# Attention and two MoE stages on one core: one pair's sums on VectorE, weight subtractions outside the routing chains, first keys in two PSUM tiles

## The chip, the cores and the metric

The kernel runs on one core of one Trainium2 chip. The metric is the device time of one execution in microseconds (us); lower is better. Inside the core five engines work side by side and meet through semaphores: TensorE (PE, matmuls and transposes), VectorE (DVE), ScalarE (ACT), GpSimd (POOL) and SyncE (SP, which only issues DMAs here). Matmul results land in PSUM, everything else lies in SBUF.

## The reference

Three steps, each on what the one before it gave:

```python
# 1 attention with random features, 16 heads (2 x 8) of 576 rows x 64
k_p, q_p = phi(k), phi(q)            # exp(x @ omega.T - sq - max) / sqrt(m), 128 features
kv, z = k_p.T @ v, k_p.sum(rows)     # per head
x = (q_p @ kv) / (q_p @ z + 1e-6)    # -> 1152 tokens x 512
# 2 MoE: 8 experts, top 1, room for 288 tokens each
logits = x @ w_gate; e = argmax(logits); gate = softmax(logits)[e]
y = relu(disp[e] @ w1[e]) @ w2[e]    # 512 -> 1024 -> 512
x = gate * y[e, pos]                 # dropped tokens give 0
# 3
h = max(x @ w1, x @ w2, x @ w3)      # 512 -> 768
out = h @ w_out                      # 768 -> 512
```

## The kernel before, in words

The order of the work is written out by hand: every engine runs its instructions in the order in which the program emits them, and an instruction whose input is not ready holds up all behind it on its engine. A list `fill` of generators (routing, transposes and lists) is advanced by one piece at each `step()`, so that their work falls between the matmuls of the main stream.

**Attention.** Two heads make a pair; there are eight pairs (`NPR`), four for each half of the tokens (`b` = 0, 1). Per pair, `proj` (L237) projects keys (s = 0) and queries (s = 1) on omega into PSUM, four tiles of 128 rows for each head, and `proj_half` the last 64 rows. `minimum` (L254) takes the row minimum on VectorE, L256, and `feature` (L258) the exponential on ScalarE, L261. `sums` (L286) adds the four key tiles of each head, L293 and L295, on the engine that the letter in the table `SUMS` (L45) names: VectorE for pair 0, GpSimd for the others. `kv_mm` (L297, matmuls L302) builds the 64 x 128 product, `z_mm` (L312) uses the sums, `q_t` (L330) transposes the query features into `qps` (L334) and ScalarE copies them out, `num` (L340) forms numerator and denominator, divides on VectorE (L356 to L379) and writes the rows into X. `keep` sends X to DRAM as XD.

**Routing.** `route(b, ...)` (L427) runs once for each half: logits, argmax, one-hot, counts by a matmul `rp` (L454), a chain of small VectorE instructions (L461 to L513) that chooses an expert and gives each token a place, five comparisons `pm` (L516, one per token tile), 15 matmuls `vps` (L534) that turn them into row indices, the indices (L558, L559), and three indirect DMAs on GpSimd (L543) that gather the rows of the expert from XD. `expert_reg` reads the expert's number into SP's register and issues the loads of its weights. The first routing is spread over pairs 5 to 7, the second over the end of the attention and the first expert's matmuls. `route_rest` picks the small third expert; its list needs the matmuls at L610. `transpose_rows` (L832) turns the gathered rows with PE into `tps` (L837), four tiles of three transposes each; ScalarE casts xth, VectorE subtracts xtl (L829).

**Experts.** Weights come as 512 KB pieces. `split` (L776) makes of a piece `raw` a rounded `hi` (ScalarE, L785) and the rest `lo` (VectorE, L788); with `split(True)` the subtraction goes into a list `rest`, from which `split_rest` takes one. `stage1` (L842) multiplies by w1 in three products (hi·hi, hi·lo, lo·hi: L140 to L142), ScalarE takes hh, VectorE takes hl (L860); `stage2` by w2. One unit of a stage is 12 matmuls of 288 columns. `tick` (L917) ends a unit; while `early[0]` holds it calls `pump`, and so `split`, only if at least `HOLD` units of the first expert's stage 1 are left. In stage 2 of the first expert the transposes of the second expert's rows start with unit `S0`. `job_c` does the third expert with few rows; the table `CAT` says behind which units of the second expert and of the last MoE its pieces run; in it `cy` (L1138) multiplies by the craw weights, the first half in one piece, the second in the next.

**The last MoE** computes the three products, takes the maximum and multiplies by w_out; its weights are decoded from 16-bit words (L677, L681). Rows are scattered by GpSimd at the end.

The lines that the change touches beside the tables: `proj`, `minimum` and `feature`, `first_keys` (L951), `route` at L521 and L546, and the main loop from L998 to L1041. In the main loop the pieces of the routing sit in `step()`:

```python
            step()
            step()
        else:
            a_step()
        num(i, None if more else lambda: next(r1))
```

## Time and profile before

| | us |
|---|---|
| median of 3 runs | 234.28 |
| lowest and highest | 232.54, 236.75 |
| the profiled execution's own time | 232.21 |
| its span, first to last instruction | 230.2 |
| busy: PE, DVE, ACT, POOL | 216.3, 143.7, 109.8, 51.0 |

The profile is of one execution. The span leaves out some 2 us around it. Busy times of engines overlap each other, and matmuls are pipelined, so PE's busy time includes matmuls that run slower than they could. PE's mean granted clock over the span was 0.986 of full speed.

### The profile page before, as it was taken

The page shows a single profiled execution, that of the slowest core. Times are in us where ns is not written, and L with a number is a line of the kernel's source. Part 1 is how long each engine was busy: PE and PEld are TensorE (multiplying, and loading weights), DVE is VectorE, ACT ScalarE, POOL GpSimd, SP SyncE. Part 2 cuts the span into 40 slices and gives each one's busy share as a digit, 9 for nine tenths or more (in the row PEclk, how much of TensorE's full clock was granted, in tenths as well). Part 3 has the DMA queues.
Part 4 walks back from the last instruction along what each step waited for, and adds up shares of the span by engine and source line. Part 5 has one row for each costly group of instructions (what it writes and reads, how often), then busy time and mean ns, then how long its engine had stood idle before and what let it go on. Part 6 is the DMA issues. An engine that isn't in the chain of part 4 may idle for free. (4 is left out here: it accounts for less than half of the span.)

```text
span 230.2 us, 5130 instructions
## 1 busy us (share of the span) xinstructions
PE 216.3 (94%) x1924; PEld 199.0 (86%) x1924; DVE 143.7 (62%) x379; ACT 109.8 (48%) x268; POOL 51.0 (22%) x96
## 2 busy tenths in 40 slices
PE   7899999999899999899899998999999999999970
PEld 3789998989796999888899997999999999988870
DVE  0755665888979789868898768456944552421120
ACT  2795966884779643046778657336621310000000
POOL 7022523331358021311000000131321111013120
PEclk9999999999979999999999999999999999999997
DMA  5938759991981616979978679974300000001211
GB/s 120 335 102 283 229 177 355 321 323 59 374 330 65 201 51 226 352 246 344 401 278 273 202 245 329 358 240 160 129 4 0 0 3 0 0 1 48 91 48 30
DMA packets 17613, 42.22 MB, mean 183 GB/s; under 512 B 2269, under 2 KB 8797, under 8 KB 17584
## 3 DMA queue, kind: packets, MB, share of 16 engines
q1 hardware_dynamic: 16016, 39.36, 49.2%
q0 software_dynamic: 800, 2.44, 3.1%
q8 instruction: 17, 0.28, 0.5%
q10 hardware_dynamic: 768, 0.05, 0.2%
q14 instruction: 12, 0.10, 0.1%
HBM read 34.36 MB, written 7.54 MB: 182 GB/s over the span
## 5 line engine op out<-in xcount | busy, mean ns | idle before, releaser
L788 DVE TENSOR_TENSOR lo<-raw,hi 128x1024 fp32r<-128x1024 f32 x27 | 33.4, 1242 | 17.5 <-ACT hi L785 15.4
L140 PE MATMUL m<-YH,hi 128*128 128x288 f32 (+1 forms) x144 | 43.3, 301 | 0.0
L141 PE MATMUL m<-YL,hi 128*128 128x288 f32 (+1 forms) x144 | 43.0, 299 | 0.0
L142 PE MATMUL m<-YH,lo 128*128 128x288 f32 (+1 forms) x144 | 42.9, 298 | 0.0
L785 ACT CAST hi<-raw 128x1024 fp32r<-128x1024 f32 x28 | 29.1, 1051 | 26.0 <-PE m L141 11.3
L140 PEld LDWEIGHTS m<-YH,hi 128*128 128x128 f32 x144 | 27.1, 188 | 0.4 <-issue 0.4
L142 PEld LDWEIGHTS m<-YH,lo 128*128 128x128 f32 x144 | 27.1, 188 | 0.0
L141 PEld LDWEIGHTS m<-YL,hi 128*128 128x128 f32 x144 | 27.1, 188 | 0.0
L261 ACT ACTIVATE kp<-ps,mn 128x128 f32<-128x128 f32 x56 | 15.3, 382 | 16.6 <-DVE mn L256 12.1
L677 ACT CAST e<-w 128x512 f16<-128x512 bf16 x24 | 18.7, 785 | 8.8 <-DMA w<-in_wm_dram 8.1
L256 DVE TENSOR_REDUCE mn<-ps 128x4 f32<-128x512 f32 (+1 forms) x32 | 19.4, 650 | 4.3 <-PE ps L249 4.2
L141 PE MATMUL hps<-xtl,hi 128*128 128x288 f32 x64 | 19.0, 297 | 0.7 <-DVE xtl L829 0.7
L140 PE MATMUL y<-hh,hi 128*128 128x288 f32 x64 | 19.6, 306 | 0.0
L1193 DVE TENSOR_TENSOR mxt<-m,mxt 128x288 f32<-128x288 f32 (+1 forms) x24 | 11.1, 462 | 13.4 <-PE m L142 13.0
L140 PE MATMUL hps<-xth,hi 128*128 128x288 f32 x64 | 19.3, 302 | 0.0
L141 PE MATMUL y<-hl,hi 128*128 128x288 f32 x64 | 18.8, 294 | 0.0
L142 PE MATMUL y<-hh,lo 128*128 128x288 f32 x64 | 18.8, 294 | 0.0
L142 PE MATMUL hps<-xth,lo 128*128 128x288 f32 x64 | 18.8, 294 | 0.0
L249 PEld LDWEIGHTS ps<-om,qk 64*128 64x128 f32 x240 | 15.8, 206 | 3.3 <-DVE om L941 1.4
L249 PE MATMUL ps<-om,qk 64*128 64x128 f32 x240 | 17.5, 299 | 1.0 <-DMA qk<-in_qk_dram 0.6
L681 DVE SCALAR_TENSOR_TENSOR raw<-w,e 128x512 int32<-128x512 int32 x24 | 17.0, 714 | 2.3 <-ACT e L677 2.3
L1196 POOL TENSOR_TENSOR H2L<-mxt,H2H 128x288 fp32r<-128x288 f32 (+1 forms) x10 | 9.5, 948 | 38.7 <-ACT H2H L95 23.9
(231 smaller groups left out, 444.5 us busy)
## 6 DMA issues: line engine op xcount, KB each, us to landing
w<-in_wm_dram SPq DMA_DIRECT2D x18, 512.0 KB, 4.9
raw<-in_w_dram SPq DMA_DIRECT2D x16, 512.0 KB, 6.5
qk<-in_qk_dram SPq DMA_DIRECT2D x7, 640.0 KB, 4.3
craw<-in_w_dram SPq DMA_DIRECT2D x8, 512.0 KB, 9.2
w<-in_wo_dram SPq DMA_DIRECT2D x6, 512.0 KB, 4.3
va<-in_va_dram SPq DMA_DIRECT2D x8, 320.0 KB, 4.8
out_dram<-zt SPq DMA_DIRECT2D x9, 256.0 KB, 5.1
XD<-X SPq DMA_DIRECT2D x2, 960.0 KB, 6.3
```

The lines of the kernel that those rows point to most:

```text
L140: T.matmul(ps, lhsT=wh, rhs=xh, start=start, stop=False)
L141: T.matmul(ps, lhsT=wh, rhs=xl, start=False, stop=False)
L142: T.matmul(ps, lhsT=wl, rhs=xh, start=False, stop=stop)
L249: T.matmul(ps[h][:, t, :], lhsT=qk_t[i][r, s, 128 * t:128 * t + 128], rhs=om[r], start=True, stop=True, tile_position=(64 * h, 0),)
L256: V.tensor_reduce(MN[i][:, k + t0:k + t1], PJ[i, s][h][:, t0:t1, :], axis=AX.X, op=ALU.min)
L261: A.activation(dst[:, 4 * h + t, :], PJ[i, s][h][:, t, :], AF.Exp, bias=mn[:, k + t:k + t + 1], scale=-1.0)
L677: A.copy(e.bitcast(F16).rearrange("p (c two) -> p c two", two=2)[:, :, 1], src.bitcast(BF16)[:, 4:4 * WH + 4:4])
L681: V.scalar_tensor_tensor(dst.bitcast(I32), src[:, 1:2 * WH + 1:2], 13, e, ALU.logical_shift_right, ALU.bitwise_or)
L785: A.copy(hi, raw)
L788: (G if SUBS[n] == "G" else V).tensor_tensor(lo, raw, hi, ALU.subtract)
L1193: V.tensor_tensor(mv, p, mv, ALU.max)
L1196: engine(HLS[k]).tensor_tensor(H2L[:, fc, n0:n1], mv, H2H[:, fc, n0:n1], ALU.subtract)
```

## The change

`SUMS[6]` becomes "V": the seventh pair's sums move from GpSimd to VectorE, and their place in the program from before the query minima to behind the two `step()` calls that end the features, ahead of `num`. In `first_keys` pair 0's key tiles t = 0, 1 get one PSUM tile and t = 2, 3 two others, and features follow each half's minima. Of the weight splits in front of the last two pairs, one subtraction is emitted at once and one is taken in the last pair, between `z_mm` and `q_th`; the last pair pumps three times in place of twice. `HOLD` = 9 stops the splits in the ticks of the first expert's stage 1, and two `split()` calls come into the second routing, behind the comparisons and behind the gathers. `S0` = 3 starts the second expert's transposes one unit earlier, and `CAT[1]` starts with 2 and 4 in place of 1 and 3, so two pieces of the third expert come one unit later.

```diff
--- before.py
+++ after.py
@@ -36,12 +36,12 @@
 W1, W2 = 2, 1
 LE, LW = 2, 3
 RA, RB, RM = 0, 1, 1
-R0, S0, LG1, LV, PMG = 4, 4, 4, (0, 3), ()
-ERX, HOLD, NB = (1, 2), 2, 2
+R0, S0, LG1, LV, PMG = 4, 3, 4, (0, 3), ()
+ERX, HOLD, NB = (1, 2), 9, 2
 WARM, CP = 7, (0, 0, 1, 1, 2)
 LI, LL = 7, 8
-CAT = (8, 12, 14), (1, 3, 5, 6)
-SUMS = "VGGGGGGG"
+CAT = (8, 12, 14), (2, 4, 5, 6)
+SUMS = "VGGGGGVG"
 KTS = "AAAAAAAA"
 QTS = "AAAAAAAAAAAAAAAA"
 QHS = "VVVVVVVV"
@@ -236,30 +236,31 @@
 
     def proj(i, s):
 
-        if (i, s) == (1, 0):
+        if i + s == 0 or (i, s) == (1, 0):
 
             nb = pn.tile([128, 2, 512], F32, tag="nb", name="nb")
             ps = [nb[:, h].rearrange("p (t m) -> p t m", m=M) for h in range(2)]
         else:
             ps = [psum([128, 4, M], f"ps{h}") for h in range(2)]
-        PJ[i, s] = ps
+        ps2 = [psum([128, 4, M], f"ps{h}") for h in range(2)] if i + s == 0 else ps
+        PJ[i, s] = (ps, ps, ps2, ps2)
         for t in range(4):
             for h in range(2):
                 r = slice(64 * h, 64 * h + 64)
                 T.matmul(
-                    ps[h][:, t, :], lhsT=qk_t[i][r, s, 128 * t:128 * t + 128], rhs=om[r], start=True, stop=True,
+                    PJ[i, s][t][h][:, t, :], lhsT=qk_t[i][r, s, 128 * t:128 * t + 128], rhs=om[r], start=True, stop=True,
                     tile_position=(64 * h, 0),
                 )
 
     def minimum(i, s, h, t0=0, t1=4):
         k = 8 * s + 4 * h
-        V.tensor_reduce(MN[i][:, k + t0:k + t1], PJ[i, s][h][:, t0:t1, :], axis=AX.X, op=ALU.min)
+        V.tensor_reduce(MN[i][:, k + t0:k + t1], PJ[i, s][t0][h][:, t0:t1, :], axis=AX.X, op=ALU.min)
 
     def feature(i, s, h, tiles=range(4)):
         mn, dst, k = MN[i], (KP, QP)[s][i], 8 * s + 4 * h
         for t in tiles:
             A.activation(
-                dst[:, 4 * h + t, :], PJ[i, s][h][:, t, :], AF.Exp, bias=mn[:, k + t:k + t + 1], scale=-1.0
+                dst[:, 4 * h + t, :], PJ[i, s][t][h][:, t, :], AF.Exp, bias=mn[:, k + t:k + t + 1], scale=-1.0
             )
 
     def proj_half(i):
@@ -519,6 +520,7 @@
         if b == 0:
             V.tensor_copy(KC[:, 0], KT[:, 0])
         if b:
+            split()
 
             expert_reg(b, NB)
         for _ in range(LV[b]):
@@ -544,6 +546,8 @@
                 rows[:n, i], None, XD[:, :], IND(IX[b][:n, i:i + 1], 0), bounds_check=2 * XR - 1, oob_is_err=False
             )
         ROWS[b] = rows
+        if b:
+            split()
         for _ in range(ERX[b] - 1):
             yield
         if b:
@@ -950,12 +954,12 @@
 
     def first_keys():
         proj(0, 0)
-        for t in (0, 2):
+        for t0 in (0, 2):
             for h in range(2):
-                minimum(0, 0, h, t, t + 2)
-        for t in range(4):
-            for h in range(2):
-                feature(0, 0, h, (t,))
+                minimum(0, 0, h, t0, t0 + 2)
+            for t in (t0, t0 + 1):
+                for h in range(2):
+                    feature(0, 0, h, (t,))
 
     def first_rest():
         proj(0, 1)
@@ -998,14 +1002,16 @@
         q_t(i, 1)
         z_mm(i)
         step()
+        if not more:
+            split_rest()
         q_th(i)
         kv_t(i)
         step()
         if i == NPR - 2:
-            for _ in range(2):
-                split(True)
+            split()
+            split(True)
         if not more:
-            for _ in range(2):
+            for _ in range(3):
                 pump()
         if more:
             if i:
@@ -1027,18 +1033,19 @@
                 if i:
                     minimum(nx, 0, h)
                 feature(nx, 0, h)
-            split_rest()
             minimum_half(nx)
             feature_half(nx)
-            sums(nx)
+            if SUMS[nx] == "G":
+                sums(nx)
             for h in range(2):
                 minimum(nx, 1, h)
                 feature(nx, 1, h)
-            split_rest()
             if i == NPR - 2:
                 split()
             step()
             step()
+            if SUMS[nx] == "V":
+                sums(nx)
         else:
             a_step()
         num(i, None if more else lambda: next(r1))
```

VectorE in the first routing. `pm` are the comparisons, `dn` is the denominator of `num`, `ks` and `ksum` are the sums. Before:

```order
L256 TENSOR_REDUCE mn<-ps_940 128x4
L513 SCALAR_TENSOR_TENSOR sm_959<-sm_959,RG 128x5
L516 TENSOR_SCALAR pm<-io,sm_959 128x288 x5
L520 COPY KC<-KT 128x8
L356 TENSOR_SCALAR dn_149<-nb 128x2x4
L357 TENSOR_SCALAR dn_149<-nb 64x2
L358 RECIPROCAL dn_149<-dn_149 128x10
```

and now:

```order
L257 TENSOR_REDUCE mn<-ps_941 128x4
L514 SCALAR_TENSOR_TENSOR sm_960<-sm_960,RG 128x5
L517 TENSOR_SCALAR pm<-io,sm_960 128x288 x5
L521 COPY KC<-KT 128x8
L294 TENSOR_TENSOR ks<-kp 128x512
L296 TENSOR_TENSOR ksum<-ks 128x256
L357 TENSOR_SCALAR dn_149<-nb 128x2x4
L358 TENSOR_SCALAR dn_149<-nb 64x2
L359 RECIPROCAL dn_149<-dn_149 128x10
```

The two sums stand between the comparisons and `num`; the rest keeps its order.

VectorE in the second routing, from hl of stage 1 (L860, now L864) to the first reduction behind the counts, before:

```order
L368 TENSOR_TENSOR X<-nb,dn_149 64x128
L860 SCALAR_TENSOR_TENSOR hl<-hps,hh 128x288
L788 TENSOR_TENSOR lo<-raw,hi 128x1024
L860 SCALAR_TENSOR_TENSOR hl<-hps,hh 128x288 x2
L788 TENSOR_TENSOR lo<-raw,hi 128x1024
L461 TENSOR_REDUCE sm_1422<-sm_1311 128x5
L462 TENSOR_SCALAR sm_1422<-sm_1422 128x5
```

and now:

```order
L369 TENSOR_TENSOR X<-nb,dn_149 64x128
L864 SCALAR_TENSOR_TENSOR hl<-hps,hh 128x288 x3
L462 TENSOR_REDUCE sm_1415<-sm_1312 128x5
L463 TENSOR_SCALAR sm_1415<-sm_1415 128x5
L464 RECIPROCAL GT<-sm_1415 128x5
```

The two subtractions (`lo`) are gone from between the hl instructions. One of them has come behind the comparisons; there stood before:

```order
L510 TENSOR_SCALAR TK<-sm_1448,sm_1442 128x8
L513 SCALAR_TENSOR_TENSOR sm_1457<-sm_1457,RG 128x5
L516 TENSOR_SCALAR pm<-io,sm_1457 128x288 x5
L860 SCALAR_TENSOR_TENSOR hl<-hps,hh 128x288 x5
L558 TENSOR_REDUCE sm_1545<-vps 128x2
L559 CAST IX_172<-sm_1545 128x2
```

and stands now:

```order
L511 TENSOR_SCALAR TK<-sm_1441,sm_1435 128x8
L514 SCALAR_TENSOR_TENSOR sm_1450<-sm_1450,RG 128x5
L517 TENSOR_SCALAR pm<-io,sm_1450 128x288 x5
L792 TENSOR_TENSOR lo<-raw,hi 128x1024
L864 SCALAR_TENSOR_TENSOR hl<-hps,hh 128x288 x5
L562 TENSOR_REDUCE sm_1542<-vps 128x2
L563 CAST IX_172<-sm_1542 128x2
```

The subtraction runs ahead of the five hl, one of which frees the PSUM buffer of `vps`.

PE in stage 2 of the first expert, one unit (12 matmuls, y tiles 1 to 4) ahead of the third expert's list (L610, now L614); before:

```order
L142 MATMUL y_1563<-hh,lo 128x288
L140 MATMUL y_1564<-hh,hi 128x288
L141 MATMUL y_1564<-hl,hi 128x288
L142 MATMUL y_1564<-hh,lo 128x288
L610 LDWEIGHTS sm_1664
L610 MATMUL vps<-VAL,sm_1664 32x6
```

and now, around the first transposes of the second expert's rows (`tps`):

```order
L140 MATMUL y_1565<-hh,hi 128x288
L141 MATMUL y_1565<-hl,hi 128x288
L142 MATMUL y_1565<-hh,lo 128x288
L841 MATMUL tps<-ident,rows 128x128 x2
L841 MATMUL tps<-ident,rows 128x32
L140 MATMUL y_1562<-hh,hi 128x288
```

The first tps no longer follows the list's matmuls at L610 but stands a unit of 12 matmuls ahead of them.

## Rows read from the trace of the kernel before

**Rows 1.** The page: busy us, share of the span and instructions of each engine

```profile
PE 216.3 (94%) x1924; PEld 199.0 (86%) x1924; DVE 143.7 (62%) x379; ACT 109.8 (48%) x268; POOL 51.0 (22%) x96
```

**Rows 2.** List of waits of PE: us in total, times, longest us

```profile
PE cy L1138 <- DMA craw<-in_w_dram: 1.0, 1, 1.0
PE vps L534 <- DVE hl L860: 0.8, 1, 0.8
PE vps L534 <- DVE pm L516: 0.8, 2, 0.5
PE qps L334 <- ACT qt L95: 0.7, 1, 0.7
PE hps L141 <- DVE xtl L829: 0.7, 1, 0.7
...
PE vps L610 <- DVE sm L603: 0.5, 1, 0.5
```

**Rows 3.** PE's time line, first pair: start us, us, instructions [idle before <- releaser]

```profile
8.45 1.96 PE L302 MATMUL kb<-kp,va 128*64 128x128 f32 x20
```

**Rows 4.** VectorE's time line: first pair's sums, then the seventh pair's stretch

```profile
10.10 0.68 DVE L293 TENSOR_TENSOR ks<-kp 128x512 f32<-128x512 f32 x1
10.82 0.42 DVE L295 TENSOR_TENSOR ksum<-ks 128x256 f32<-128x256 f32 x1
...
58.47 2.72 DVE L516 TENSOR_SCALAR pm<-io,sm 128x288 bf16<-128x288 f16 x5
...
61.19 0.15 DVE L356 TENSOR_SCALAR dn<-nb 128x8 f32<-128x8 f32 x1
...
66.07 1.29 DVE L256 TENSOR_REDUCE mn<-ps 128x4 f32<-128x512 f32 x2 [1.43 <-PE ps L249]
```

**Rows 5.** GpSimd's time line: seventh pair's sums, then the first row gathers

```profile
58.51 1.30 POOL L293 TENSOR_TENSOR ks<-kp 128x512 f32<-128x512 f32 x1 [5.03 <-ACT kp L261]
59.89 0.80 POOL L295 TENSOR_TENSOR ksum<-ks 128x256 f32<-128x256 f32 x1
64.00 1.25 POOL L543 DMA_INDIRECT rows<-XD,IX  x1 [3.31 <-DMA raw<-in_w_dram]
...
66.86 0.93 POOL L543 DMA_INDIRECT rows<-XD,IX  x1 [0.31 <-DVE mn L256]
```

**Rows 6.** PE's time line, 58 to 71 us: kv group, transposes, first tps

```profile
58.44 1.25 PE L302 MATMUL kb<-kp,va 128*64 128x128 f32 x19
...
61.69 1.09 PE L334 MATMUL qps<-ident,qp 128*128 128x128 f32 x8
...
70.19 1.16 PE L837 MATMUL tps<-ident,rows 128*128 128x128 f32 x6
```

**Rows 7.** Stretches: window, us, busy us by engine (x instructions), PEclk, DMA share, GB/s

```profile
63.00:67.00 4.00, 4.00 (x37) 3.72 (x38) 2.36 (x13) 2.49 (x4) 2.38 (x3) 0.57 1.03 399
```

**Rows 8.** Gathers of the first routing: times from issue to landing

```profile
DMA to landing us min/median/max: 3.1/4.2/4.2
```

**Rows 9.** VectorE's time line in the second routing: a subtraction, and the comparisons

```profile
87.01 1.22 DVE L788 TENSOR_TENSOR lo<-raw,hi 128x1024 fp32r<-128x1024 f32 x1
...
91.26 1.11 DVE L516 TENSOR_SCALAR pm<-io,sm 128x288 bf16<-128x288 f16 x5
```

**Rows 10.** PE's time line in the second routing and stage 2 behind it

```profile
92.79 0.61 PE L534 MATMUL vps<-VAL,pm 128*128 128x6 bf16 x15 [0.81 <-DVE hl L860]
...
97.01 0.29 PE L140 MATMUL y<-hh,hi 128*128 128x288 f32 x1
...
98.59 0.29 PE L140 MATMUL y<-hh,hi 128*128 128x288 f32 x1
...
102.02 0.41 PE L610 MATMUL vps<-VAL,sm 128*32 128x6 bf16 x10 [0.49 <-DVE sm L603]
```

**Rows 11.** Gathers of the second routing: the third issue, and times to landing

```profile
97.96 0.91 POOL L543 DMA_INDIRECT rows<-XD,IX  x1 [0.30 <-issue]
...
DMA to landing us min/median/max: 2.9/4.0/4.8
```

## The prediction

> **What bounds the kernel now.** I read the busy shares first. TensorE (PE) works through 94% of the span, VectorE 62%, so the end moves only by what PE waits for, by PE work that goes, and by PE's clock [rows 1]. The second view was PE's list of waits: one wait each for the craw DMA (1.0 us), for VectorE's hl ahead of the second routing's vps (0.8), for ScalarE's qt copy (0.7), for the last xtl (0.7) and for the list of the small third expert (0.5), and two short ones for pm (0.8 together) [rows 2]. The reader is to see that this is about 4.5 us in all. No edit can gain more through waits alone, unless PE also runs small matmuls at the pace of their inputs, which counts as busy. The start has such a place. The first kv group (L302, 20 matmuls) took 1.96 us; the same group of the seventh pair took 1.25 for 19 [rows 3, 6]. The third view was the time line of the two routings on VectorE, GpSimd and PE, since most edits stand there.
>
> All sums are made against the profiled execution, 232.2 us (span 230.2 and 2.0 around it); the median of the three runs shown is 234.28. I carry the difference in us over to the median.
>
> **Start: first keys in two tiles.** Nothing is added; the first half of the minima no longer shares a tile with projections that wait for the second piece of the load, so the first features begin earlier. The last features of the group still come after the half-tile's minimum. The cap is 1.96 less about 1.3, so 0.7 us; nothing is a possible end too, as the next pair's keys come from a load of their own. I take 0.4, near the middle, because the group's last matmul needs the half-tile's feature, which doesn't move.
>
> **Seventh pair's sums.** GpSimd loses two instructions (1.30 and 0.80 us) [rows 5], VectorE gets them at 0.68 and 0.42, its durations for the first pair [rows 4]. In return the five comparisons (pm, L516), which took 2.72 us while GpSimd's sums ran beside them, should take the 1.11 that the same five took in the second routing with GpSimd idle [rows 4, 5, 9]. The row shows a slowing by 2.45 times under a busy GpSimd. The Trainium skill (SBUF — State Buffer, section Who interferes with whom) says that VectorE and GpSimd share a pair of ports by an exclusive lock which a VectorE tensor_scalar may need; the trace agrees in direction, 1.6 us beside 2.1 us of GpSimd work. The same section has a two-input VectorE addition contend with a GpSimd instruction that reads SBUF; the moved sums are such additions, but no GpSimd instruction stands beside them, so the sum by that rule is the one above.
>
> VectorE's own chain to the row indices thus changes by -1.61 + 1.10, about -0.5 us: L356, before at 61.19, starts near 60.7. On PE the 15 vps matmuls no longer trickle: from the end of L302 (58.44 + 1.25 = 59.7) to the transposes (61.69) passed 2.0 us [rows 6], and the same 15 took 0.61 in the second routing [rows 10]: 1.4 less. That isn't all kept. PE's next use of the routing is tps at 70.19, just behind the landing of the third gather (issued 66.86 and, by the shortest of the three durations, 3.1 later: 69.96) [rows 5, 6, 8]. The gathers hang on VectorE's indices and move by 0.5 only, so PE comes to tps at 68.8 and stands until 69.7. In the stretch before, the granted clock was 0.57 over 4 us, that is 3.4 us at the lower level (1.2 GHz) and 1.7 us lost [rows 7]. If that drop goes with the shorter trickle, PE comes even earlier (67.1) and waits longer, to the same 69.7. Kept: 0.5 us. The ends: nothing, and 1.1 if the gathers also land faster, because one 512 KB weight load is now queued on SP behind the write of X and no longer runs beside them (the three landed in 4.2, 4.2 and 3.1; 2.9 is the shortest of the second routing) [rows 8, 11].
>
> **Subtractions out of the chains.** Each L788 is 1.22 us of VectorE [rows 9] and none goes or is added. In the last pair one now runs ahead of the eighth pair's minima, where VectorE idled 1.43 us for PE's projections anyway [rows 4], and one behind the four xtl. The wait for qt (0.7) [rows 2] goes, since the second transpose now takes a PSUM buffer that a tps left, freed by VectorE early: -0.7, or nothing if another buffer is late in its place. What could come late is a weight's lo; PE's list has no wait for one [rows 2], so I count nothing, and up to 1.2 us, one L788, if that lead were gone.
>
> In the second routing the two L788 between the hl's and L461 go, and one returns between pm and the five hl's. The indices come 2.4 us earlier relative to PE's stream at most, and the hl that frees vps' PSUM buffer by 1.2. PE arrives earlier by what was won before, so of the 0.8 I count 0.3 as gone; the ends are 0.8 and -0.5 (a loss, if the L788 in front of hl decides).
>
> **S0 from 4 to 3.** The first transposes of the second expert's rows come 12 matmuls earlier, 1.58 us (from 97.01 to 98.59) [rows 10]. PE came to L610 at about 101.5 (102.02 less its wait), so it will stand at tps at 101.5 - 1.58 = 99.9 in the old frame. The third gather was issued at 97.96 and landed 2.9 later, at 100.86 [rows 11]. With the gathers and PE both moved by the same 1.9 us a new stall of 0.9 us appears: +0.9. Ends: 0 (the chain wins the whole 2.4 and PE less) and 2.8 (gathers don't move). In return the wait at L610 (0.5) goes, since the transposes fill it, and the wait for xtl (0.7) goes, since the last xtl no longer stands behind an L788 at the end of stage 2: -1.2, ends -1.2 and 0.
>
> **CAT.** The second half of cy comes one unit (1.58 us) later, behind the same craw load. If the load moved with PE the wait of 1.0 would be gone. It is issued on SP behind weight loads which follow VectorE and DMA rather than PE. If it stays where it is while PE is 3.1 us early, the wait is 1.0 + 3.1 - 1.6 = 2.5. I take -0.5, ends -1.0 and +1.5.
>
> **Sum.** -0.4 - 0.5 - 0.7 - 0.3 + 0.9 - 1.2 - 0.5 = -2.7 us. Behind cy PE's list has no further wait [rows 2], so this reaches the end. Profile about 229.5 us; median 234.28 - 2.7 = 231.6 us.
>
> **Rivals.**
> - *A new low stretch of the clock.* The stall at the first tps is 0.9 to 2.6 us, longer than the 0.8 that stood ahead of the old low stretch [rows 2, 7]. If the clock falls after it as it did at 63 us, 1.7 us of real work is lost: -2.7 + 1.7 = -1.0, 233.3 us. Against it: the 1.0 at craw was not followed by a low stretch. [...]
> - *The comparisons stay slow.* If pm's 2.72 us came from something other than GpSimd (the DMA engines were full there), the sums only lengthen the chain: the gathers come 1.1 later instead of 0.5 earlier, so -2.7 + 1.6 = -1.1, 233.2 us. The change then doesn't do what it says. Against it: the same five took 1.11 in the second routing.
> - *Everything is kept.* The gathers land early enough for both tps, craw is on time: -0.7 - 1.1 - 0.7 - 0.8 + 0 - 1.2 - 1.0 = -5.5, 228.8 us. For it: less DMA beside the first gathers. Against it: three gathers are issued one after the other on GpSimd, 3.8 us from the first start (64.00) to the last end (66.86 + 0.93), and that order stays [rows 5].
> - *Slower.* The low clock outlasts the stall at the first tps: PE goes on with small matmuls of the last pair. Each us at the lower level costs 0.5. It decides from 5.4 us on, where the -2.7 is used up; at 10 us it gives +2.3, 236.6 us. Against it: the old stretch ended after 3.4 us amid matmuls of that kind.
>
> **How the numbers follow.** Chances: forecast 0.46 (its own range 230.0 to 232.8), new low stretch 0.17, slow comparisons 0.09, everything kept 0.21, slower 0.07. The range goes from 228.0 to 235.0: it holds nearly all of the first three and the greater part of the fourth. A measurement of this kernel tells about 2%, 4.7 us, from no change: below 229.6 lies the better part of "everything kept" and a little of the forecast, 0.25; above 239.0 only a very long low clock, 0.04; within, 0.71.
>
> **What would show it.** Right: pm x5 near 1.1 us in the first routing, with the two sums behind it on VectorE; vps x15 near 0.6; a PE wait at the first tps; no PE wait for qt, L610 and xtl; a short wait at the first tps of the second expert; cy's wait below 1 us. Wrong: pm still above 2 us; PE idle above 2 us at the second tps or at cy; a low clock behind 70 us; a new wait of PE on lo.

## The result, and the profile after

| | us |
|---|---|
| median of 4 runs of the changed kernel | 230.37 (229.06 to 231.34) |
| median of before | 234.28 (232.54 to 236.75) |
| ratio, with its 95% interval | 0.9859 (0.9811 to 0.9907) |
| forecast | 231.6 (228.0 to 235.0) |
| profiled execution: time, span | 230.97, 229.2 |

The change gains 3.3 us by the ratio, 3.9 by the medians; 2.7 were forecast. The two profiled executions differ by 1.2 us only, since the one of after ran its first 10 us at TensorE's lower clock (below). The comparisons by ratio leave out executions more than 1.5% above the fastest of their kernel, and with them those in which TensorE's clock was low for long, so the medians of all executions stand beside the ratios.

PE's waits after (us in total, times, longest), where rows 2 showed craw, qt, xtl, pm and the list:

```profile
PE tps L841 <- DVE sm L598: 1.7, 1, 1.7
PE tps L841 <- DMA rows<-XD,IX: 1.4, 4, 0.5
...
PE cz L1156 <- DVE pc L1153: 0.9, 1, 0.9
PE vps L536 <- DVE hl L864: 0.5, 1, 0.5
```

All waits of [rows 2] but one are gone (hl went from 0.8 to 0.5), and three lines are new, 4.0 us together: 1.1 us at the first transposes (tps) of the first expert's rows, 2.0 at those of the second, and 0.9 at cz. The "sm" in the first line is only the semaphore that came last by the records; in the profiles of e8 and e9 the same wait is put down to the gathers.

The seventh pair's stretch on PE, beside [rows 6]:

```profile
59.13 1.25 PE L303 MATMUL kb<-kp,va 128*64 128x128 f32 x19
60.32 0.61 PE L536 MATMUL vps<-VAL,pm 128*128 128x6 bf16 x15
...
63.08 2.06 PE L250 MATMUL ps<-om,qk 64*128 64x128 f32 x32
...
68.50 0.30 PE L841 MATMUL tps<-ident,rows 128*128 128x128 f32 x1 [0.45 <-DMA rows<-XD,IX]
69.19 0.33 PE L841 MATMUL tps<-ident,rows 128*128 128x128 f32 x1 [0.38 <-DMA rows<-XD,IX]
69.83 0.79 PE L841 MATMUL tps<-ident,rows 32*128 32x32 f32 x4 [0.31 <-DMA rows<-XD,IX]
```

and on VectorE, beside [rows 4]:

```profile
59.16 1.11 DVE L517 TENSOR_SCALAR pm<-io,sm 128x288 bf16<-128x288 f16 x5
...
60.26 0.69 DVE L294 TENSOR_TENSOR ks<-kp 128x512 f32<-128x512 f32 x1
60.98 0.42 DVE L296 TENSOR_TENSOR ksum<-ks 128x256 f32<-128x256 f32 x1
61.32 0.16 DVE L357 TENSOR_SCALAR dn<-nb 128x8 f32<-128x8 f32 x1
```

The comparisons take 1.11 us in place of 2.72, the two sums follow at 0.69 and 0.42, and vps x15 takes 0.61 right behind the kv group. The 32 projections at 63 us run at the upper clock (2.06 us). PE then comes to tps early and waits three times, 1.14 us in all, for one gather after the other. GpSimd's first and last gather, and the times to landing, beside [rows 5, 8]:

```profile
64.15 1.24 POOL L545 DMA_INDIRECT rows<-XD,IX  x1 [9.96 <-DMA raw<-in_w_dram]
...
67.13 0.93 POOL L545 DMA_INDIRECT rows<-XD,IX  x1 [0.31 <-issue]
...
DMA to landing us min/median/max: 2.7/3.0/3.4
```

They go out no earlier than before (64.15 against 64.00, the start having cost 0.7 us). The 2.7 and 3.4 us are those of the third and the second gather, in place of 3.1 and 4.2; the landing of the first is not on record. The first tps waits for it and starts at 68.50. In six profiles that have the record (e2 to e6, e8), that tps starts 0.13 or 0.14 us behind the landing, so by my estimate the first gather took some 4.2 us, as it did before.

The order of the DMAs on SP around these gathers, before and after (`raw` are the 512 KB weight loads, `XD<-X` is the write of X):

```profile
55.74 3.77 SPq L718 DMA_DIRECT2D raw<-in_w_dram  x7
72.90 0.40 SPq L184 DMA_DIRECT2D XD<-X  x1
```

```profile
56.44 3.20 SPq L722 DMA_DIRECT2D raw<-in_w_dram  x6
70.06 0.40 SPq L184 DMA_DIRECT2D XD<-X  x1
70.69 1.46 SPq L722 DMA_DIRECT2D raw<-in_w_dram  x2
```

The seventh load now goes out behind the write of X, 14 us after the others of its group began. The moves of the subtractions in the pair loop bring this about: e5, without them, has the old order, and e10, with them alone, the new one.

The second routing on PE, beside [rows 10], and its gathers on GpSimd, beside [rows 11]:

```profile
90.90 0.61 PE L536 MATMUL vps<-VAL,pm 128*128 128x6 bf16 x15 [0.47 <-DVE hl L864]
...
99.74 0.30 PE L841 MATMUL tps<-ident,rows 128*128 128x128 f32 x1 [1.68 <-DVE sm L598]
100.31 0.57 PE L841 MATMUL tps<-ident,rows 128*128 128x128 f32 x2 [0.27 <-DMA rows<-XD,IX]
...
102.61 0.41 PE L614 MATMUL vps<-VAL,sm 128*32 128x6 bf16 x10
```

```profile
93.35 1.54 POOL L545 DMA_INDIRECT rows<-XD,IX  x1 [7.34 <-DVE IX L563]
...
96.50 0.91 POOL L545 DMA_INDIRECT rows<-XD,IX  x1 [0.30 <-issue]
...
DMA to landing us min/median/max: 4.1/4.6/5.1
```

vps starts 1.9 us earlier than before. 1.5 of this is PE's lead at the matmuls of the counts (85.23 against 86.77). The comparisons start 3.0 us behind these in place of 4.5, but vps only 5.7 in place of 6.0, as it still waits for hl. Nearly all of the lead ends at the first tps: a wait of 1.68 us, then 0.27. The first gather is issued 1.9 us earlier (93.35 against 95.24), but its issue takes 1.54 us in place of 1.11. The second and the third need 5.1 and 4.1 us to land in place of 4.0 and 2.9; the first, again without a record, some 6.3 by the same estimate in place of 4.8.

The start of this execution, and that of a later one with the same first keys (run e6):

```profile
5.60 3.06 PE L250 MATMUL ps<-om,qk 64*128 64x128 f32 x24
8.60 1.12 PE L272 MATMUL psh<-om,qk 64*64 64x128 f32 x8
9.64 1.61 PE L303 MATMUL kb<-kp,va 128*64 128x128 f32 x20
```

```profile
6.47 1.16 PE L250 MATMUL ps<-om,qk 64*128 64x128 f32 x16 [0.26 <-DMA qk<-in_qk_dram]
7.56 0.65 PE L272 MATMUL psh<-om,qk 64*64 64x128 f32 x8
8.14 1.44 PE L303 MATMUL kb<-kp,va 128*64 128x128 f32 x20
```

The same eight psh matmuls took 1.12 us in one and 0.65 in the other. The clock records tell why. In the profile of the changed kernel the first record of the granted clock stands at 10.30 us. Up to there the first pair's projections take 418 ns each, behind it those of the next pair 272. In e6 the first record stands at 4.20, and all take 272. A window ahead of the first record is shown with a clock of 1.00 only because nothing is recorded there. In e9 a record covers the psh:

```profile
8.70 1.12 PE L272 MATMUL psh<-om,qk 64*64 64x128 f32 x8
8.70:9.82 1.12, 1.12 (x12) 0.79 (x12) 0.00 (x0) 0.21 (x1) 0.00 (x0) 0.50 0.76 290
```

It is 0.50, the lower level (1.2 GHz), with the same 1.12 us. So the slow start is the lower clock. The first record lies between 4.2 and 5.3 us in six of the 14 profiles and between 8.5 and 10.3 in eight. PE did the same ahead of it in all (seven matmuls into `wps`, from 1.05 to 4.22), and both the old first keys (before, e4, e10) and the new ones are found in both groups.

### The profile page after: what moved, and what is told of

Its sections match the earlier page's. It is cut to its first block, busy times and chain, and to the rows that moved or that the text cites. A ratio compares the mean times of both kernels' runs of the same rounds, so it can differ in the third digit from the quotient of the medians.

```text
span 229.2 us, 5130 instructions
## 1 busy us (share of the span) xinstructions
PE 216.2 (94%) x1924; PEld 199.2 (87%) x1924; DVE 144.4 (63%) x381; ACT 109.1 (48%) x268; POOL 48.2 (21%) x94
## 5 line engine op out<-in xcount | busy, mean ns | idle before, releaser
L792 DVE TENSOR_TENSOR lo<-raw,hi 128x1024 fp32r<-128x1024 f32 x27 | 33.8, 1258 | 16.6 <-ACT hi L789 16.5
L262 ACT ACTIVATE kp<-ps,mn 128x128 f32<-128x128 f32 x52 | 14.2, 383 | 12.5 <-DVE mn L257 10.6
L257 DVE TENSOR_REDUCE mn<-ps 128x4 f32<-128x512 f32 (+1 forms) x30 | 18.7, 666 | 1.4 <-PE ps L250 1.0
L685 DVE SCALAR_TENSOR_TENSOR raw<-w,e 128x512 int32<-128x512 int32 x24 | 17.6, 738 | 2.1 <-ACT e L681 2.1
L262 ACT ACTIVATE qp<-ps,mn 128x128 f32<-128x128 f32 x64 | 17.8, 443 | 0.0
L250 PE MATMUL ps<-om,qk 64*128 64x128 f32 x232 | 16.6, 295 | 0.0
```

The source lines that it names most:

```text
L250: T.matmul(PJ[i, s][t][h][:, t, :], lhsT=qk_t[i][r, s, 128 * t:128 * t + 128], rhs=om[r], start=True, stop=True, tile_position=(64 * h, 0),)
L257: V.tensor_reduce(MN[i][:, k + t0:k + t1], PJ[i, s][t0][h][:, t0:t1, :], axis=AX.X, op=ALU.min)
L262: A.activation(dst[:, 4 * h + t, :], PJ[i, s][t][h][:, t, :], AF.Exp, bias=mn[:, k + t:k + t + 1], scale=-1.0)
L685: V.scalar_tensor_tensor(dst.bitcast(I32), src[:, 1:2 * WH + 1:2], 13, e, ALU.logical_shift_right, ALU.bitwise_or)
L792: (G if SUBS[n] == "G" else V).tensor_tensor(lo, raw, hi, ALU.subtract)
```

## The experiments

Each kernel is the changed one with the edit shown, except e10, which is the one of before with an edit. The kernel of before, run beside each group, had medians of 233.5 to 234.3 us. Median clock is that of the mean granted clock over a run's executions; the time ahead of the first clock record counts as full clock in it.

| run | median us (executions, of these in the ratio) | ratio to before, interval | median clock |
|---|---|---|---|
| changed kernel | 230.4 (4, 4) | 0.986 (0.981 to 0.991) | 0.986 |
| e1 sums back | 231.1 (6, 4) | 0.983 (0.976 to 0.991) | 0.979 |
| e2 S0 back | 230.8 (6, 5) | 0.986 (0.981 to 0.992) | 0.984 |
| e3 all split moves back | 234.2 (12, 10) | 1.001 (0.998 to 1.005) | 0.975 |
| e4 first keys back | 233.9 (6, 2) | 0.988 (0.979 to 0.997) | 0.970 |
| e5 pair loop's split moves back | 235.6 (13, 5) | 0.998 (0.993 to 1.003) | 0.964 |
| e6 routing's split moves back | 230.8 (6, 5) | 0.986 (0.980 to 0.992) | 0.986 |
| e7 fill ahead of the first tps | 230.0 (6, 6) | 0.986 (0.981 to 0.991) | 0.990 |
| e8 split behind the gathers | 231.0 (6, 5) | 0.989 (0.983 to 0.995) | 0.980 |
| e9 as e5, with the new load order | 231.3 (6, 4) | 0.984 (0.978 to 0.989) | 0.982 |
| e10 pair loop's split moves alone | 232.7 (12, 12) | 0.995 (0.992 to 0.999) | 0.983 |
| e11 CAT back | 231.5 (6, 5) | 0.989 (0.983 to 0.994) | 0.987 |
| e12 fill, last X write on GpSimd | 231.3 (12, 10) | 0.989 (0.985 to 0.993) | 0.986 |

**e1.** Sums on GpSimd again:

```diff
-SUMS = "VGGGGGVG"
+SUMS = "VGGGGGGG"
```

> The changed kernel with one edit undone: the seventh pair's sums are on GpSimd again (SUMS[6] = G, emitted where they were). Theory (GpSimd's sums slow the comparisons beside them): the five comparisons of the first routing take about 2.7 us again in place of 1.11, vps x15 trickles over 1.5 to 2.0 us in place of 0.61, and the time is 0.5 to 1.5 us above the changed kernel's 230.4, more by 1.7 if the low stretch of TensorE's clock near 63 us comes back with the trickle. Rival (the comparisons were slow for another reason, full DMA engines or their place): they stay near 1.1 us and the time stays within 0.5 us of the changed kernel.

The comparisons on VectorE, and vps and the projections on PE:

```profile
57.70 2.71 DVE L517 TENSOR_SCALAR pm<-io,sm 128x288 bf16<-128x288 f16 x5
```

```profile
60.06 0.92 PE L536 MATMUL vps<-VAL,pm 128*128 128x6 bf16 x13 [0.49 <-DVE pm L517]
...
63.09 3.46 PE L250 MATMUL ps<-om,qk 64*128 64x128 f32 x32
```

The mechanism is shown: 2.71 us beside GpSimd's sums, 1.11 without. The trickle of vps and the low clock come back with it (the projections take 3.46 us), yet the time doesn't move beyond the interval: PE now comes to tps at 69.4, when the rows are there, without a wait. Trickle and low clock fill the time that the stall would take, so the gain that the sums' move was to keep is not seen.

**e2.** S0 as before:

```diff
-R0, S0, LG1, LV, PMG = 4, 3, 4, (0, 3), ()
+R0, S0, LG1, LV, PMG = 4, 4, 4, (0, 3), ()
```

> The changed kernel with S0 = 4 again: the second expert's first transposes come one unit (12 matmuls, 1.58 us) later, behind the third expert's list. Theory (the new stall of 1.7 us at the first tps is the price of S0 = 3, since the gathers don't come earlier): that stall shrinks to 0.1 us or less, but the list's matmuls wait about 1.4 us instead, since the reduction chain in front of them on VectorE hangs on a weight load that lands near 97 us, and the last xtl may wait 0.5 again; the time is within 0.7 us of the changed kernel. Rival (S0 = 3 pays as forecast, 1.2 gained for 0.9): the time is 0.3 to 1.0 us above. Second rival (S0 = 3 costs more than it gives): 0.7 to 1.5 us below the changed kernel.

Two of PE's waits in its profile:

```profile
PE vps L614 <- DVE sm L607: 1.4, 1, 1.4
...
PE hps L141 <- DVE xtl L833: 0.7, 1, 0.7
```

The stall at the second expert's first tps is gone, and these two stand in its place: 2.1 us against 1.95. The time is the same; S0 moves a wait.

**e3.** All split moves undone (the edits of e5 and e6 together).

> The changed kernel with the moves of the weight subtractions undone: HOLD = 2, no split inside the second routing, the last two pairs' splits as before; sums, first keys, S0 and CAT stay changed. Theory (the subtractions were in the second routing's chain and ScalarE's qt copy held up the transposes): the wait for qt (0.7 us) comes back, two L788 stand again in front of the second routing's chain, the comparisons there start 1 to 1.5 us later relative to PE, the gathers too, and the stall at the second expert's first tps grows from 1.9 to 2.9 us or more; the time is 1.5 to 2.5 us above the changed kernel. The first gathers run beside one more 512 KB load and take 4.2, 4.2, 3.1 us in place of 3.4, 3.0, 2.7. Rival (the chain isn't what the gathers of the second routing wait for, their DMA is): the stall stays near 1.9 and the time is at most 0.8 us above.

The first gathers' landing:

```profile
DMA to landing us min/median/max: 3.7/4.8/5.7
```

The whole gain is gone, more than any theory gave. The stall at the second expert's tps did not grow (0.5 and 0.25 us); the loss lies at the first tps, where PE waited 1.9 us and then ran at 1.2 GHz for 6.8 of the next 16 us. e5, e6 and e9 take this apart.

**e4.** The first pair's keys as before:

```diff
-        if i + s == 0 or (i, s) == (1, 0):
+        if (i, s) == (1, 0):
...
-        for t0 in (0, 2):
+        for t in (0, 2):
             for h in range(2):
-                minimum(0, 0, h, t0, t0 + 2)
-            for t in (t0, t0 + 1):
-                for h in range(2):
-                    feature(0, 0, h, (t,))
+                minimum(0, 0, h, t, t + 2)
+        for t in range(4):
+            for h in range(2):
+                feature(0, 0, h, (t,))
```

> The changed kernel with the first pair's keys in two PSUM tiles of four row tiles each and the old order of minima and features. Theory (the start gains 0.4 us and the slow matmuls of the first 9 us in the changed kernel's profile are chance): time 0.2 to 0.6 us above the changed kernel, and the start's matmuls run at either pace in any kernel. Rival (the new order keeps the start's clock low): the first pair's projections run at full pace again, psh x8 in 0.65 us in place of 1.12, and the kernel is 0.5 to 1.0 us faster than the changed one.

The rival falls: the start was at the lower clock with the old order too (psh x8 in 1.11 us). The ratio is 0.2% above the changed kernel's, well within the intervals, but it rests on two executions. The median lies 3.5 us higher because the other four had a mean clock of 0.970 or less. Of the 58 executions of the nine kernels with the new keys and the new load order (the changed one, e1, e2, e6 to e9, e11, e12) only four had that, so chance alone is a poor account; how the first keys would bring it is not shown, and what they are worth stays open.

**e5.** The pair loop's split moves undone:

```diff
-        if not more:
-            split_rest()
         q_th(i)
...
-            split()
-            split(True)
+            for _ in range(2):
+                split(True)
         if not more:
-            for _ in range(3):
+            for _ in range(2):
                 pump()
...
+            split_rest()
             minimum_half(nx)
...
+            split_rest()
             if i == NPR - 2:
```

> The changed kernel with the split moves in the attention loop undone and those in the second routing kept. On VectorE this puts two L792 back among the eighth pair's minima and takes one from behind the four xtl; on SP the write of X stands again behind the seventh weight load, not ahead of it. Theory (the first gathers run beside one more weight load and land late, PE stands at the first tps for 1.9 us or more and its clock falls behind the stall): most of the 3.4 us of the run with all split moves undone comes from here; time 1.5 to 3 us above the changed kernel's 230.4; the first gathers take 3.7 to 5.7 us. Rival (the gain sits in the second routing's chain): time within 0.7 us of the changed kernel.

The first tps on PE, the first gathers' landing, and the stretch behind (columns as in [rows 7]):

```profile
69.47 0.30 PE L841 MATMUL tps<-ident,rows 128*128 128x128 f32 x1 [1.83 <-DMA rows<-XD,IX]
70.02 1.58 PE L841 MATMUL tps<-ident,rows 128*128 128x128 f32 x5 [0.24 <-DMA rows<-XD,IX]
```

```profile
DMA to landing us min/median/max: 3.6/4.7/5.6
```

```profile
68.00:84.00 16.00, 13.55 (x68) 11.19 (x68) 9.04 (x19) 8.28 (x18) 4.80 (x3) 0.57 0.34 113
```

This edit holds the gain: 0.998 in place of 0.986, or 2.9 us; by the medians 5.2, more than the theory gave. The three gathers land 5.6, 4.7 and 3.6 us after their issues, as in e3, and PE waits 1.83 us for the first. In this execution, one of the longer ones (237.97 us), the clock is 0.57 over 16 us: 13.7 us at the lower level, a loss of up to 6.9; e3's, of 234.09 us, has 6.8 us. The mean clock was 0.970 or less in nine of e5's 13 executions and four of e3's 12.

**e6.** The second routing's split moves undone:

```diff
-ERX, HOLD, NB = (1, 2), 9, 2
+ERX, HOLD, NB = (1, 2), 2, 2
...
-            split()
 
             expert_reg(b, NB)
...
-        if b:
-            split()
```

> The changed kernel with HOLD = 2 and without the two splits inside the second routing; the attention loop stays changed. Two L792 (1.22 us each) stand again in front of the second routing's chain on VectorE, none behind the comparisons and none beside the gathers. Theory of the forecast (each L792 delays the chain): the comparisons start 2.4 us later relative to the counts' matmul, the gathers 1.2 us later or more, and the stall at the second expert's first tps is 1 us longer: 0.5 to 1.5 us above the changed kernel. Rival (the gathers then run without an L792 beside them, their first issue takes 1.1 in place of 1.5 us, and they land nearly as early): time within 0.5 us of the changed kernel.

The rival holds. The comparisons start 4.6 us behind the counts in place of 3.0, but vps only 0.4 later relative to them. The first gather went out in 1.06 us with no L792 beside it and the stall at tps was 1.10 us in place of 1.68; vps waited 0.9 in place of 0.5. The sum is nearly the same (2.0 and 2.2), and so is the time.

**e7.** Work without a result in the stall:

```diff
             ps = psum([128, SA], "tps")
+            if b == 0 and j == 0:
+                for _ in range(12):
+                    T.transpose(ps[:, 0:128], ident, ident)
```

> The changed kernel with 12 more transposes of the identity (fp32, 128 x 128) on TensorE ahead of the first tps, into the part of its PSUM tile that is overwritten behind them: work without a result, in the time in which PE waits for the gathers. Theory (the idle stretch in front of the first tps is what lets the clock fall behind it, in some executions): no low clock between 68 and 85 us in the profile, the mean clock of the timed executions is higher and the time 0.5 to 2 us lower than the changed kernel's, with less spread. Rival (the clock falls whatever PE does there): same spread, and the time is 0 to 1 us higher, as 12 transposes take 1.6 us and the stall is 1.1 to 1.5.

```profile
68.03 1.53 PE L842 MATMUL tps<-ident 128*128 128x128 f32 x12
69.40 0.41 PE L844 MATMUL tps<-ident,rows 128*128 128x128 f32 x2
70.11 0.79 PE L844 MATMUL tps<-ident,rows 32*128 32x32 f32 x4 [0.29 <-DMA rows<-XD,IX]
```

```profile
68.00:84.00 16.00, 15.71 (x133) 14.44 (x132) 14.02 (x36) 10.86 (x29) 5.88 (x5) 1.00 0.43 146
```

The 12 transposes take the place of the wait, of which 0.29 us is left, and no low clock follows. That fits the theory, but the changed kernel's own profile shows no low clock there either. The median clock is the highest of all runs (0.990 against 0.986 in four executions), the spread is no smaller (2.7 us against 2.3), and the median time is only 0.3 us below the changed kernel's: a gain, if there is one, is smaller than the runs can tell.

**e8.** The second split of the second routing behind the tails:

```diff
         ROWS[b] = rows
-        if b:
-            split()
...
         tails(b, ps[:32, 2:3], slice(64 - 64 * b, 96 - 64 * b), slice(2, 3))
+        if b:
+            split()
         yield
```

> The changed kernel with the second split of the second routing emitted behind the tails of the routing, not between the gathers and the tails; one L792 on VectorE thereby starts some 2 us later. Theory (that L792 runs while GpSimd issues the first gather and slows it from 1.1 to 1.54 us): the first gather of the second routing takes 1.1 us, the third is issued 0.4 us earlier, the stall at the second expert's first tps is 0.4 us shorter; time 0 to 0.5 us lower. Rival (the gathers' landing is set by the weight loads beside them): the stall stays, time unchanged.

The first gather's issue, and the subtraction beside it:

```profile
93.38 1.06 POOL L545 DMA_INDIRECT rows<-XD,IX  x1 [7.67 <-DVE idt L567]
93.40 1.23 DVE L792 TENSOR_TENSOR lo<-raw,hi 128x1024 fp32r<-128x1024 f32 x1
```

The issue takes 1.06 us in place of 1.54, as the theory said, though L792 came only 0.7 us later and still runs beside it: it now starts just behind the gather, not ahead of it. And yet the stall stays (1.60 and 0.27): the three landed after 4.5 to 6.2 us. So the issue does not set the gathers' end. That the weight loads beside them do, as the rival says, fits; no run moved these loads.

**e9.** The old order on VectorE (e5), with the seventh weight load held back on SP until the write of X is issued:

```diff
+            if count["load"] == 6 and not gate[0]:
+                return
...
             keep(i // NP, slice(0, 384))
+            if i > NP:
+                gate[0] = True
+                load_more()
```

> The kernel of the run with the attention loop's split moves undone, but with the seventh weight load held back until the write of X is issued: SP's order is that of the changed kernel, VectorE's is the old one (two L792 among the eighth pair's minima, none behind the xtl). It tells the two effects of those moves apart. Theory (the load beside the first gathers makes them late, the long stall brings the low clock): the gathers take 2.7 to 3.5 us again, the stall at the first tps is about 1.1 to 1.3 us, and 2 to 3.5 of the 3.4 us come back: 230.5 to 232 us. Rival (VectorE's order decides: minima and features of the eighth pair late, xtl late, the wait for qt): time stays at 233 us or above, with the wait for qt of 0.7 us.

```profile
69.32 0.30 PE L845 MATMUL tps<-ident,rows 128*128 128x128 f32 x1 [0.94 <-DMA rows<-XD,IX]
69.86 1.05 PE L845 MATMUL tps<-ident,rows 128*128 128x128 f32 x5 [0.24 <-DMA rows<-XD,IX]
...
74.55 0.66 PE L335 MATMUL qps<-ident,qp 128*128 128x128 f32 x4 [0.73 <-ACT qt L95]
```

```profile
DMA to landing us min/median/max: 2.7/3.3/3.8
```

```profile
68.00:84.00 16.00, 14.09 (x104) 12.43 (x105) 12.22 (x30) 8.85 (x20) 6.90 (x5) 0.89 0.44 150
```

One DMA's place on a queue brings the gain back: 0.984 in place of e5's 0.998. The third and the second gather land after 2.7 and 3.8 us in place of 3.6 and 4.7; the first, without a record, took some 4.7 by the estimate above (issued at 64.47, its tps at 69.32) in place of 5.6. The stall is 0.94 in place of 1.83, and the clock over the same 16 us is 0.89. The wait for qt (0.73) is there as in e5, so it is the order on VectorE that brings it; in the time it is not seen. The low clock is rarer, not gone: one of the six executions had a mean clock below 0.970 (0.951, 239.58 us), and in the profile 3.4 us at the lower level begin at 75.8, behind the wait for qt.

**e10.** The pair loop's split moves (the reverse of e5's diff) on the kernel of before.

> The kernel of before with the attention loop's split moves alone (they bring the load order on SP with them); sums on GpSimd, first keys, S0, HOLD and CAT as before. Theory (these moves carry nearly all of the gain): ratio to before 0.985 to 0.991, no wait for qt; TensorE comes to the first tps without a stall because the trickle of vps and the low clock near 63 us stay. Rival (they pay only where the sums' move has made TensorE early): ratio 0.995 to 1.0.

0.5%, at the near end of the rival's range; the interval leaves the theory's out: no wait for qt, no stall at tps, but the trickle and the low clock at 63 us stay, and the waits for hl (0.9), xtl (1.4 in two) and craw (1.4) are as large as before or larger. With the sums on GpSimd in both, e1 is 1.2% faster than this one. So the other edits (first keys, S0, the routing's splits, CAT) do count together, though by the ratios none of them is told from nothing alone in e2, e4, e6 and e11. The rival's reason, TensorE made early by the sums' move, is not what is missing: e1 has its gain without it.

**e11.** CAT as before:

```diff
-CAT = (8, 12, 14), (2, 4, 5, 6)
+CAT = (8, 12, 14), (1, 3, 5, 6)
```

> The changed kernel with CAT[1] = (1, 3, 5, 6): the third expert's cy pieces one and two units earlier again. Theory (the new wait of 0.9 us for pc at cz is the price of the later second piece, and takes back what the craw wait gives): cy waits up to 1 us for craw again, cz waits 0 to 0.3 us, time within 0.5 us of the changed kernel. Rival (the forecast: 0.5 us gained by CAT): 0.3 to 0.8 us above it.

0.3% above the changed kernel, which leans to the forecast (0.5 us) but lies within the intervals. In the profile neither craw nor cz was waited for, so the exchange of waits that I expected isn't shown; it had 10 us of low clock at 70 to 80 us, which may have made all loads early relative to PE (not shown).

**e12.** The fill of e7, and X's last write on GpSimd's queue:

```diff
-            keep(i // NP, slice(384, 512))
+            keep(i // NP, slice(384, 512), G if i > NP else SP)
```

> The changed kernel with the 12 filling transposes ahead of the first tps and with the last write of X (320 KB) issued from GpSimd's queue. SP then no longer stands some 9 us in front of the first loads of the last MoE's weights, which go out near 75 to 81 us in place of 86, while the DMA engines are idle, and are through before the second routing's gathers. Theory (the weight traffic beside them makes the second gathers late): they take 2 to 3.5 us in place of 4.1 to 5.1, the stall at the second expert's first tps falls from 1.2 to 1.9 us to below 1.0; time 228.5 to 230 us. Rival (the two expert loads behind the routing are what runs beside them): the stall stays, time as with the fill alone.

One of SP's waits, of the first loads of the last MoE:

```profile
SPq L675 <- DMA XD<-X: 14.6, 1, 14.6
```

A miss. These loads were issued from 86.5 us on, as before (86.1 in the changed kernel), because they wait for the write of X to land, whichever queue issues it: it went out at 83.1 and landed at 86.2, in the changed kernel 83.3 and 85.9. So the traffic beside the second gathers was not moved, and the theory stays untested. In the profile two of these gathers took 5.2 and 6.2 us (the first has no record), PE waited 3.0 us for them, and the clock was at the lower level for 10.2 us behind that wait.

**The clock behind the first tps, over all profiles.** With the sums on VectorE and no fill, PE waited 1.0 us or more in all at the first tps in nine kernels. In eight the granted clock fell to the lower level afterwards, in seven of them within 2.6 us, in e9 after 6.5 and behind the wait for qt. It stayed there for 3.4 us (e2, e6, e8, e9), 6.8 in two pieces (e3), 10.2 (e4, e11) or 13.7 (e5). The length does not follow the wait: e4 and e11 had waited 1.0 and 1.1 us, e2 1.5, e3 and e5 2.2 and 2.1. In the changed kernel's own profile it did not fall. With the fill (e7, e12) it did not fall there either. With the sums on GpSimd (before, e1, e10) there was no wait at tps and the low stretch lay at 62 to 67 us, 3.4 us in each. At the second expert's first tps, PE waited 1.0 us or more in all in seven profiles; the clock fell in four (e1, e5, e8, e12) and not in the changed kernel, e6 and e7. The Trainium skill (TensorE: Matmul & The Clock Gate, section HAM oscillation) tells of a kernel in which waits for data between bursts of matmuls bring the lower level back each time; its waits are longer than those here. In this case's traces shorter waits were followed by it too, in eight kernels of nine at the first tps.

## Why the prediction was right or wrong, step by step

The sum was right: -2.7 forecast, -3.3 by the ratio (-2.2 to -4.4 by its interval), with the time inside the range. Its terms were not, and that they add up is in good part luck: one is worth four times its size, and three show nothing that the runs can tell.

**Subtractions out of the pair loop** was the step that was mis-sized. The forecast gave it 0.7 us for qt, and put the load that no longer runs beside the gathers at the far end of another term (1.1 us). The runs give it about 1.2% of the time, 2.9 us (e5 against the changed kernel), and in e9 the load's place on SP alone brings that back, with the wait for qt still there. The price is not the 0.9 us of longer waiting alone. The median clock is 0.964 in e5 and 0.982 in e9; over 234 us that is some 4 us by my estimate, about the difference of the two medians (235.6 and 231.3). Why the clock is low in more executions with the old load order is not shown, as the length of the low stretches does not follow the wait. The new low stretch was a rival of mine, at 0.17 and for the changed kernel. What I didn't see is that it comes more often without the new load order than with it, since I counted the old load order's cost on the kernel of before. There it was small: its first gather took 4.2 us with the old order, the changed kernel's some 4.2 with the new one, and all the moves in the pair loop together are worth 0.5% on that kernel (e10).

**Seventh pair's sums:** the mechanism came as forecast (comparisons in 1.11 us, vps in 0.61, a stall of 1.1 within the 0.9 to 2.6), and "the comparisons stay slow" is out by e1. The 0.5 us that it was to keep is not seen: e1 is as fast.

**Second routing's splits (-0.3):** nothing, by e6. The wait for hl did go from 0.8 to 0.5 us, as the step said, and comes back in e6 (0.9). But the 1.5 us that the comparisons gained on the counts were only 0.35 at vps, and the longer stall at tps took that.

**S0 (+0.9 - 1.2):** both halves are real, but of the same size. The stall was 2.0 us, not 0.9. PE came as forecast (98.1 against 98.0), but the third gather went out 0.4 us later, behind the longer issue of the first, and took 4.1 us to land; I had carried over the shortest duration of before, 2.9. e2 gives no difference.

**CAT (-0.5):** 0.65 us by the two ratios, within their intervals. craw's wait went as forecast, but e11 has none with the old table either, so it is not shown that CAT took it away; the wait of 0.9 us at cz was not foreseen. The far end of this term was also added up wrong: with the new stall of 0.9, PE would have been 2.2 us early there, not 3.1.

**Start (-0.4):** with the upper clock in both, the first kv group ends at 9.58 (e6: 8.14 + 1.44) in place of 10.41 [rows 3], 0.8 us earlier, more than my cap, because the projections ahead of it also run earlier: PE waited 0.6 us for the second piece of the load before, 0.26 in e6. My 4.5 us of waits had left out that one and 0.5 for om. In starts at the lower clock little is left of it (11.42 in e4, 11.33 in e3). In time e4 shows 0.2%, which is not told from none.

"Everything is kept" did not come: the gathers of both routings still land later than PE gets there, the second ones later after their issue than before. "Slower" is not the changed kernel, but e5's profiled execution shows that its mechanism exists: 13.7 us of low clock, at 237.97 us.

## What to carry to other kernels

When a chain ends in a small gather, look at what else is on the DMA engines when it is issued: here one 512 KB load moved behind the write of X on SP was worth more, in the changed kernel, than any other of its edits. When an edit turns a trickle of small matmuls into a clean wait, price the clock behind the wait, not the wait alone. Filling the wait kept the clock up there in both profiles in which it was tried, but no gain in time could be told. And where several edits trade one wait for another, undo them one at a time before believing any term of the sum.

## What was not expected of the hardware

- At the start, TensorE's clock rose to the upper level at 4.2 to 5.3 us in six of 14 profiles and at 8.5 to 10.3 in eight, after the same work; the kv group of the first pair ended at 9.58 us in e6 and at 11.25 in the changed kernel's profile.
- A gather's issue on GpSimd took 1.54 or 1.55 us in the nine profiles in which a VectorE subtraction of two SBUF operands (L792, 1.23 us) had started 0.6 us ahead of it, and 1.06 to 1.12 in four without one. In e8, where L792 started 0.02 us behind it and ran beside it, it took 1.06. In e10 the second gather of the first routing took 1.48, with a subtraction started 0.6 us ahead of it, and 1.00 before. So it matters which of the two starts first.
- In all eight profiles that have both records, the first gather of the first routing landed 0.6 to 1.5 us behind the last weight load issued ahead of it on SP. In e5 the last of these loads land 1.3 us apart.
- Low stretches of the clock behind waits of 1.0 to 2.2 us at the first tps lasted from 3.4 to 13.7 us in kernels that differ from the changed one by a single undone group of edits; what sets the length is open.
